# Reordering a fused attention and long-convolution kernel: the long kernel's transform ahead of the v projections, its spectra beside the logits

## The chip, the cores and the metric

The kernel runs on one core of one Trainium2 chip. The metric is the device time of one execution in microseconds (us). Times are medians over several executions of the same build, each beside executions of the kernel before on the same chip. Engine names in the profile: PE is TensorE (matmuls), PEld its weight loads, DVE is VectorE, ACT is ScalarE, POOL is GpSimd, SP is SyncE (here only a DMA queue). L582 means line 582 of the kernel source. In the traces here an engine's work stands in compiled order behind whatever waits ahead of it (DVE once for 8.84 us, below), and this matters for all that follows.

## The reference

Two unrelated computations share a launch, on sequences of 2048 rows with 576 columns:

```python
# A: dilated sliding-window attention, 32 heads of 18, window 8, dilation 2
q, k, v = split(x @ wqkv)
logits  = einsum("bhsd,bhswd->bhsw", q, k[idx]) * 18 ** -0.5   # idx = s - 2*w, masked below 0
o       = einsum("bhsw,bhswd->bhsd", softmax(logits), v[idx])
a       = o @ wo
# B: H3 long convolution
kv  = shift_conv4(k, shift_k) * v
y   = irfft(rfft(pad(kv)) * rfft(pad(ssm_k)))[:2048] + kv * ssm_D
b   = q * y
return concatenate([a, b], axis=-1)
```

`ssm_k` is called the long kernel below; it is as long as the sequence, so its transform costs as much as that of the data.

## The kernel before

The program is a string of 302 steps. Each step is `name.arguments:modifiers`; the modifiers choose which pair of PSUM buffers the step uses (`a` or `b`) and which engine copies the result out of PSUM (`s` ScalarE, `v` VectorE). A loop over the string emits instructions, and the framework's scheduler then fixes an order for each engine.

```python
for item in ORDER.split():
    item, _, mods = item.partition(":")
    name, *args = item.split(".")
    how["ps"] = next((m for m in mods if m in "ab"), None)   # PSUM pair
    how["ev"] = next((m for m in mods if m in "vs"), None)   # evacuating engine
    STEP[name](*map(int, args))
```

The steps that matter:

| step | what it does | lines |
|---|---|---|
| `v` | one of 16 v projections, ten matmuls | L380 |
| `lm`, `lb` | logit products on DVE; the sum of one of 8 groups on PE | L500, L516 |
| `kt`, `kp` | transpose of the long kernel and first transform stage, written to DRAM as `Dk` | L429 |
| `kl`, `xl` | load of a tile of `Dk` or `Dx` into a ring of slots | L568 |
| `ks`, `xs` | a spectrum: eight matmuls, four evacuations | L563 |
| `gp`, `gi` | spectral product on DVE; inverse stage on PE | L582, L596 |
| `pm`, `ps` | attention product on DVE; its sum on PE | L618, L632 |

A k spectrum has a tail that an x spectrum does not have. The product needs each half of it on the other half's partitions too, and two DMA copies on the POOL queue make that copy:

```python
def w_load(Dd, key, i):
    nc.sync.dma_start(Wr.get((key, i)), by_rt(Dd, i // 4, i % 4))

def k_spec(i):
    Kc = Kr.get(i)
    s2(Wr[("k", i)], i % 4, Kc[:, 0], 1.0 / 2048)      # matmuls and evacuations
    Wr.drop(("k", i))
    nc.gpsimd.dma_start(Kc[0:64, 1], Kc[64:128, 0])    # L574: the swap
    nc.gpsimd.dma_start(Kc[64:128, 1], Kc[0:64, 0])    # L575

def g_prod(i, hv):                                     # L582, needs Kc[:, 0] and Kc[:, 1]
    nc.vector.tensor_tensor(Pp.get((i, hv)), Kr[i][:, :, 4 * hv:4 * hv + 4, :],
                            Xr[i][:, 4 * hv:4 * hv + 4, :].unsqueeze(1).to_broadcast([128, 2, 4, HD]), ALU.mult)
```

In the string of before, all of `kl`, `ks`, `xl`, `xs` come behind the last group sum `lb.7`.

## Time and profile before

| | before |
|---|---|
| time, median of the first three executions | 253.45 us |
| span of the profiled execution | 251.1 us |
| PE busy | 222.8 us (89%) |
| DVE busy | 206.9 us (82%) |
| mean granted PE clock | 0.969 of full |

The prediction shows the page's busy shares and slices and the hole between 120 and 144 us. Two more views of the same run are needed. The first is the table of busy times over stages: window in us, its width, then busy time and instruction count of PE, PEld, DVE, ACT and POOL, the granted clock, the DMA share, and GB/s.

```profile
6.28:113.00 106.72, 104.11 (x799) 58.84 (x806) 100.26 (x118) 81.58 (x104) 5.49 (x18) 1.00 0.59 184
113.00:129.45 16.45, 14.53 (x132) 8.62 (x124) 12.42 (x16) 8.81 (x12) 1.49 (x2) 1.00 0.79 225
129.45:146.00 16.55, 8.21 (x44) 4.70 (x41) 11.80 (x13) 10.16 (x16) 1.08 (x2) 0.61 0.88 242
146.00:163.22 17.22, 15.42 (x180) 12.79 (x179) 13.26 (x13) 11.75 (x21) 2.05 (x4) 0.98 0.94 272
```

Subtract busy from width. PE has one bad row, the third: 8.3 us idle. DVE has three: 4.0, 4.8 and 4.0 us idle, 12.7 in all. The eye goes to PE's hole, since it is deep; DVE's is shallower and longer, and larger in sum.

The second is the list of waits: engine, line and what was waited for; then total us, how often, and the longest.

```profile
PE psB L563 <- DMA area<-Dx: 6.9, 2, 4.8
DVE area L582 <- DMA area<-area: 6.5, 4, 2.4
```

There are two candidates of the same size. PE waits for the load of `Dx`; DVE waits for the swap of a k spectrum. Nothing in these two lines says which of them sets the end. (Not all of DVE's idle time is the swap's: of the 4.8 us in the third row, 2.36 are put down to the swap and 2.03, ahead of the first attention product at 135.34 us, to another DMA between SBUF tiles, by its place a halo copy of v from the SP queue.)

### The profile page before, as it was taken

The page shows a single profiled execution, that of the slowest core. Times are in us where ns is not written, and L with a number is a line of the kernel's source. Part 1 is how long each engine was busy: PE and PEld are TensorE (multiplying, and loading weights), DVE is VectorE, ACT ScalarE, POOL GpSimd, SP SyncE. Part 2 cuts the span into 40 slices and gives each one's busy share as a digit, 9 for nine tenths or more (in the row PEclk, how much of TensorE's full clock was granted, in tenths as well). Part 3 has the DMA queues.
Part 4 walks back from the last instruction along what each step waited for, and adds up shares of the span by engine and source line. Part 5 has one row for each costly group of instructions (what it writes and reads, how often), then busy time and mean ns, then how long its engine had stood idle before and what let it go on. Part 6 is the DMA issues. An engine that isn't in the chain of part 4 may idle for free.

```text
span 251.1 us, 4991 instructions
## 1 busy us (share of the span) xinstructions
PE 222.8 (89%) x2007; PEld 150.5 (60%) x2013; DVE 206.9 (82%) x232; ACT 161.0 (64%) x231; POOL 25.4 (10%) x62
## 2 busy tenths in 40 slices
PE   1999899999999999999872599799999998999991
PEld 1346645445475549576531288667887786778881
DVE  2889999999997889998956679699889898966433
ACT  2878966765887756986645585688898653551120
POOL 8800000000000000002001011011120111111000
PEclk9999999999999999999996589999999999999998
DMA  6999994420336173918799779889978899968974
GB/s 206 328 337 373 357 310 125 162 87 28 94 97 188 27 210 94 273 33 241 210 223 318 226 196 283 276 244 271 287 234 228 291 247 255 322 212 263 276 228 141
DMA packets 44366, 55.24 MB, mean 220 GB/s; under 512 B 2316, under 2 KB 37468, under 8 KB 44344
## 3 DMA queue, kind: packets, MB, share of 16 engines
q1 hardware_dynamic: 42374, 47.71, 62.8%
q0 software_dynamic: 1968, 7.23, 10.7%
q8 instruction: 15, 0.25, 0.4%
q14 instruction: 7, 0.06, 0.1%
q10 hardware_dynamic: 2, 0.00, 0.0%
HBM read 29.27 MB, written 18.87 MB: 192 GB/s over the span
## 4 chain that ended last, share of the span: by engine, by line
PE 59%; DMA 10%; issue 10%; ACT 8%; DVE 7%; SPq 2%; POOL 1%; DVEq 0%; ACTq 0%; POOLq 0%
PE psA L393 10%; ACT area L96 8%; PE psA L380 7%; DMA area<-area 6%; PE psA L516 5%; PE psA L632 5%; PE psB L393 4%; PE psA L651 4%; PE psB L429 4%; PE psB L651 3%; DMA Dk<-area 2%; DVE area L618 2%; DMA area<-in_A_x_dram 2%; PE psB L596 2%; PE psB L632 1%
## 5 line engine op out<-in xcount | busy, mean ns | idle before, releaser
L96 ACT ACTIVATE area<-psB 128x576 bf16<-128x576 f32 (+6 forms) x124 | 84.6, 714 | 42.3 <-PE psB L563 13.4
L96 ACT ACTIVATE area<-psA 128x576 bf16<-128x576 f32 (+6 forms) x91 | 66.1, 753 | 38.7 <-PE psA L632 12.3
L618 DVE TENSOR_TENSOR area<-area,area 128x4096 bf16<-128x4096 bf16 x16 | 36.6, 2285 | 6.2 <-DMA area<-area 2.0
L500 DVE TENSOR_TENSOR area<-area 128x2048 bf16<-128x2048 bf16 x32 | 38.0, 1223 | 3.1 <-PE psA L516 3.1
L632 PEld LDWEIGHTS <-area 128*128 128x128 bf16 x512 | 32.6, 99 | 2.6 <-issue 0.5
L632 PE MATMUL psA<-ident,area 128*128 128x128 bf16 x448 | 32.0, 222 | 0.2 <-ACT area L96 0.2
L563 PE MATMUL psB<-area,W 128*128 128x288 bf16 x104 | 21.5, 306 | 9.4 <-DMA area<-Dx 6.9
L393 PEld LDWEIGHTS <-area 128*128 128x128 bf16 x160 | 15.8, 100 | 19.6 <-issue 3.2
L393 PE MATMUL psA<-area,area 128*128 128x512 bf16 x105 | 27.1, 401 | 0.2
L582 DVE TENSOR_TENSOR area<-area,area 128x2304 bf16<-128x2304 bf16 x16 | 21.2, 1350 | 6.5 <-DMA area<-area 6.5
L380 PEld LDWEIGHTS <-area 128*128 128x128 bf16 x160 | 19.7, 145 | 6.3 <-issue 5.7
L563 PEld LDWEIGHTS <-W 128*128 128x128 bf16 x128 | 12.6, 105 | 17.9 <-DMA area<-Dx 7.9
L380 PE MATMUL psA<-wv,area 128*128 128x288 bf16 x160 | 22.2, 288 | 0.9 <-ACT area L96 0.8
L460 DVE TENSOR_TENSOR area<-area,area 128x2304 bf16<-128x2304 bf16 x16 | 21.3, 1351 | 0.9 <-DMA area<-in_B_k_dram 0.8
L662 POOL DMA_DIRECT2D area<-in_B_q_dram x8 | 6.1, 765 | 133.9 <-DVE area L500 105.6
L651 PEld LDWEIGHTS <-area 128*128 128x128 bf16 x160 | 15.4, 97 | 5.8 <-issue 1.0
L429 PE MATMUL psB<-area,T 128*128 128x384 bf16 x74 | 17.2, 326 | 1.0 <-DVE area L290 0.4
L465 DVE TENSOR_TENSOR area<-area 128x2304 bf16<-128x2304 bf16 x12 | 16.2, 1352 | 0.2
L672 DVE TENSOR_TENSOR area<-psB,area 128x576 bf16<-128x576 f32 x13 | 9.6, 752 | 8.0 <-PE psB L671 5.7
L516 PE MATMUL psA<-area,Eh 128*32 128x512 bf16 x112 | 15.7, 632 | 0.0
L596 PEld LDWEIGHTS <-IAt 128*128 128x128 bf16 x128 | 12.2, 97 | 5.6 <-issue 2.5
L651 PE MATMUL psA<-wv,area 128*128 128x288 bf16 x90 | 13.3, 286 | 1.0 <-DVE area L98 0.7
(121 smaller groups left out, 274.2 us busy)
## 6 DMA issues: line engine op xcount, KB each, us to landing
Dx<-area SPq DMA_DIRECT2D x16, 288.0 KB, 3.0
Dk<-area SPq DMA_DIRECT2D x16, 288.0 KB, 4.4
area<-Dk SPq DMA_DIRECT2D x8, 576.0 KB, 4.9
area<-Dx SPq DMA_DIRECT2D x8, 576.0 KB, 5.6
area<-area POOLq DMA_DIRECT2D x16, 288.0 KB, 6.3
Dy<-area SPq DMA_DIRECT2D x8, 576.0 KB, 4.5
out_dram<-area SPq DMA_DIRECT2D x16, 288.0 KB, 4.6
area<-Dy SPq DMA_DIRECT2D x8, 576.0 KB, 6.6
```

The lines of the kernel that those rows point to most:

```text
L96: nc.scalar.activation(dst, src, ACT.Copy, **({} if scale is None else {"scale": scale}))
L380: nc.tensor.matmul(ps[:, di, 0:288], xTt[:, kb, t2, :], wv[:, kb, d0:d1], start=(kb == 0), stop=(kb == 4))
L393: nc.tensor.matmul(ps[:, u, :], wcols(kb, comp, 2 * cp + u), xT[:, kb, t], start=(kb == 0), stop=(kb == 4))
L429: nc.tensor.matmul(ps[:, ri, 0:384], T1[:, ri, :], sf[:, 384 * ch:384 * ch + 384], start=True, stop=not extra)
L460: nc.vector.tensor_tensor(dst, kfull[:, 4 * c + 3 - j:4 * c + 7 - j, :], skb[:, j, :].unsqueeze(1).to_broadcast([128, 4, D]), ALU.mult)
L500: nc.vector.tensor_tensor(dst[:, u], halves(q2[h], hf), halves(k2[h][:, :, shs[u]:shs[u] + S], hf), ALU.mult)
L516: nc.tensor.matmul(psw[32 * j:32 * j + 32, 0, :].rearrange("p (u a b) -> p u a b", u=2, b=2), Eh[:, 2 * h + c, :], prr[(n, h)][:, :, c, :, ...
L563: nc.tensor.matmul(ps[:, hp, 0:HD], W2[:, 8 * g + 2 * prl + hp].rearrange("p i l f -> p (i l f)"), Wt[:, 2 * prl + hp, :], start=True, sto ...
L582: nc.vector.tensor_tensor(Pp.get((i, hv)), Kr[i][:, :, 4 * hv:4 * hv + 4, :], Xr[i][:, 4 * hv:4 * hv + 4, :].unsqueeze(1).to_broadcast([12 ...
L618: nc.vector.tensor_tensor(P.rearrange("p w (d h) -> p w d h", h=H), vs[:, :, 0:16], at.to_broadcast([128, W, 16, H]), ALU.mult)
L632: nc.tensor.matmul(oaccs[tp][:, u, ct, :], P[:, wi, 128 * ct:128 * ct + 128], ident[:], start=(ct == 0 and wi == 0), stop=(wi == W - 1 and ...
L651: nc.tensor.matmul(ps[:, di, 0:288], lhs, wot[:, ct if ct < 4 else 4 + u, d0:d1], start=(ct == 0), stop=(ct == 4))
```

## The change

The intent is to end the transform of the long kernel early, beside the first logit groups, and to keep the v projections for later. Then loads and spectra (with their swaps) can be issued while logits are still summed, and PE has projections to fill the latency. The string is new throughout; its core is here, with cuts marked.

```diff
-lm.2.2 kp.1.2:s lb.2:s v.7:sa lm.3.1 lm.3.2 lm.4.0 kp.2.0:s kp.2.1:s lb.3:as kt.3:vb kp.2.2:a lm.4.1 v.6:a kt.4:bv
 [...]
-kp.6.1:sb kp.6.2:s v.14:s lm.6.1 kp.7.0:bs v.15:s kp.7.1:bs lm.6.2 lb.6:s lm.7.0 v.12:a lm.7.1 kp.7.2:b lwo ha.2 ha.3
-lm.7.2 lb.7:av kl.0 xl.0 ks.0:b kl.1 xl.1 xs.0 ks.1:a kl.2 pm.0.0 xs.1:b pm.0.1 xl.2 gp.0.0 gi.0.0 gp.0.1 ks.2:sb
+kp.7.1:s lm.3.2 lb.3:va sa.0 kp.7.2:b v.8:sb lm.4.0 v.4:as lm.4.1 lm.4.2 v.6:bs kl.0 v.5 kl.1 v.7 lm.5.0 lb.4:a lm.5.1
+lm.5.2 ks.0:bs lb.5:bs ha.1 v.11:a lm.6.0 sb.0 v.10:a ks.1:sa v.14:as xl.0 lm.6.1 v.12:bv v.13:va v.15:bs xl.1 v.9:sa
+lm.6.2 lb.6:av xs.1:b ha.2 lm.7.0 kl.2 ha.3 lm.7.1 at.0:s xs.0:sb lm.7.2 xl.2 lb.7 gp.0.0 gp.0.1 gi.0.0:b pm.0.0
 [... the rest of the string also changes in order, PSUM pair and evacuating engine]
-    Wr = Ring(mk.take(8, HD), mk.take(8, HD), wx)
+    Wr = Ring(mk.take(8, HD), mk.take(8, HD))
+    left = {f"v.{i}" for i in range(NT)} | {...all qk and qt steps...}
     for item in ORDER.split():
         [...]
+        left.discard(item)
+        if not left and len(Wr.slots) == 2:
+            Wr.slots.append(wx)
```

The last part is a matter of memory: the third load slot `wx` lies over the transposed x, which the projections read, so it joins the ring only when the last projection has been emitted.

More of the change, by code (lines that the diff above doesn't have):

```diff
@@ L18 @@
 ORDER = """
-lx.0 lwq.0 lx.2 xt.0.0:bs lx.1 sk:b lwq.1 xt.0.1:sa lkv.0 lkv.1 xt.0.2:v qk.0.1.0:bs cv.0 qk.0.0.0:sa lx.3 qk.1.0.0
-xt.1.0:bs xt.1.2:v lkv.2 xt.1.1:s qk.1.1.0:sa xt.2.0:a ia xt.2.2:s wt:s xt.3.2:va xt.3.0:b xt.3.1:sa sx.0.0:av cv.1
-sx.0.1:a sx.0.2:s qk.0.1.1 sx.1.0:b qk.0.0.1:a sx.1.1:sb sx.1.2:s lwv qk.1.0.1 cv.2 qk.1.0.3:sb xt.2.1:sa sx.2.0:sb
-lkv.3 sx.2.1:b qk.1.1.1:sa sx.2.2 sx.3.0:av qk.0.0.3:sb sx.3.1:v qt.0:bs qk.0.1.2:s sx.3.2:s qk.1.0.2:bs qk.1.1.2:av
-sx.4.0:s qk.0.0.2:sb cv.3 sx.4.1:b v.1:s qt.2:b sx.4.2:a qt.1:bs sx.5.0:b qk.0.1.3:s qk.1.1.3:sa sx.5.1 sx.5.2:v
@@ L24 @@
-qt.3:sa v.2:a v.0:a sx.6.0:a sx.6.1:sb sx.6.2:s lm.0.0 lm.0.1 sx.7.0:b lkn sx.7.1 kt.0:a lm.1.0 sx.7.2 lm.0.2 lb.0
-v.4:a lm.1.1 lm.2.0 kp.0.0:sb kp.0.1:a kt.1:s lm.1.2 lb.1:a lm.2.1 v.3:a kp.0.2:a kt.2:vb kp.1.0:as lm.3.0 kp.1.1:as
-lm.2.2 kp.1.2:s lb.2:s v.7:sa lm.3.1 lm.3.2 lm.4.0 kp.2.0:s kp.2.1:s lb.3:as kt.3:vb kp.2.2:a lm.4.1 v.6:a kt.4:bv
-kp.3.0:b v.5 ha.0 sa.0 kp.3.1:b kp.3.2:vb v.8:as kp.4.0:sb kp.4.1:s lm.4.2 kp.4.2:bs kt.5:v ha.1 sb.0 kt.6:a lb.4:as
-v.9:s v.10:s lm.5.0 v.11:a kp.5.0 kp.5.1:bs lm.5.1 lm.5.2 kp.5.2 kp.6.0:a at.0:s lb.5:bs kt.7:bv lm.6.0 v.13:va
@@ L29 @@
-kp.6.1:sb kp.6.2:s v.14:s lm.6.1 kp.7.0:bs v.15:s kp.7.1:bs lm.6.2 lb.6:s lm.7.0 v.12:a lm.7.1 kp.7.2:b lwo ha.2 ha.3
-lm.7.2 lb.7:av kl.0 xl.0 ks.0:b kl.1 xl.1 xs.0 ks.1:a kl.2 pm.0.0 xs.1:b pm.0.1 xl.2 gp.0.0 gi.0.0 gp.0.1 ks.2:sb
-xs.2:vb gp.1.0 xl.3 sa.1 xl.4 pm.1.0 gi.0.1:s gp.1.1 gp.2.0 ps.0.0:as ps.0.1:s ps.1.0:s xs.3 kl.3 ks.3:sb gi.1.0:bs
-kl.4 pm.1.1 gi.1.1:b ps.1.1:as gp.2.1 gp.3.0 pm.2.0 gi.2.0:av ks.4:s sb.1 xl.5 xs.4:s gi.2.1 po.0.0 kl.5 po.0.1:sb
-ps.2.0:v gp.3.1 gp.4.0 pm.2.1 ks.5:b ps.2.1:b po.1.0:bs pm.3.0 xs.5:a po.1.1:as gi.3.0:sb gi.3.1:bs kl.6 at.1 gp.4.1
@@ L34 @@
-pm.3.1 ps.3.0:a ps.3.1:a gi.4.0:sa pm.4.0 gi.4.1:sa gp.5.0 xl.6 ks.6:as xs.6:b yl.0 gp.5.1 pm.4.1 po.2.0:sb gp.6.0
-gi.5.0:v ys.0.0 pm.5.0 po.2.1:sa xl.7 kl.7 ks.7:v ps.4.0:as yl.1 pm.5.1 xs.7:sb po.3.0:v ps.4.1:sa ys.0.1:b po.3.1:sb
-yl.2 yl.3 gi.5.1:a ps.5.0:a pm.6.0 gp.6.1 gp.7.0 ys.1.0 ys.1.1 gi.6.0:bs gi.6.1:a ys.2.0:b ps.5.1:b gi.7.0:a ys.2.1
-gp.7.1 pm.6.1 po.4.0:sb gi.7.1:s yl.4 yl.5 ys.3.0:b po.4.1:v po.5.0:b ys.3.1:b ps.6.0:bv ps.6.1:av po.5.1:bs pm.7.0
-pm.7.1 po.6.0:s yl.6 ys.4.0:a ps.7.0:s ys.4.1 ys.5.0:a yl.7 po.6.1:av ys.5.1 ps.7.1:s ys.6.0:b po.7.0:a po.7.1:s
@@ L39 @@
-ys.6.1:b ys.7.0:b ys.7.1:a
+lx.0 xt.0.0:va xt.0.1:sa lx.1 lwq.0 sk:b lx.2 xt.0.2:a lwq.1 lkv.0 lkv.1 qk.0.0.0:sa qk.0.1.0:bs cv.0 lx.3 xt.1.2:sa
+xt.1.1:s lkv.2 xt.1.0:b qk.1.0.0:s ia:sb sx.0.0:b qk.1.1.0:sa xt.3.0 cv.1 sx.0.1:sa xt.2.0:a xt.3.2:v qk.0.0.1:av
+sx.0.2 xt.2.1:sb wt:s sx.1.0:bs sx.1.1:av qk.0.1.1:s xt.3.1:sb sx.1.2:as cv.2 qk.1.0.1:bs qt.0:bs sx.2.0:s xt.2.2:av
+sx.2.1:b lkv.3 qk.1.0.3 qk.0.0.3:sa sx.2.2:b sx.3.0:bs qk.1.1.1:as sx.3.1 lwv qk.0.1.2:a lkn qt.1:as sx.3.2:sb
+qk.1.0.2:s sx.4.0:bs qt.3 sx.4.1:av cv.3 sx.4.2:sb v.1:bs qt.2 v.2:sb sx.5.0:bv sx.5.1:as sx.5.2:as qk.0.0.2:b
@@ new lines @@
+qk.0.1.3:s sx.6.0:s sx.6.1 qk.1.1.3:a sx.6.2:b qk.1.1.2:b kt.0:a lm.0.0 sx.7.0:sa sx.7.1:v kp.0.0:sa sx.7.2:s kt.1:vb
+kp.0.1:sb kp.0.2:av v.0:sb kt.2:sa lm.0.1 lm.1.0 lm.0.2 kp.1.0:as kp.1.1:av kp.1.2:s lb.0:sb kp.2.0:a kp.2.1:s lm.1.1
+kt.3:v kp.2.2:as kp.3.0:s kt.4:va lm.1.2 kp.3.1:a lm.2.0 kp.3.2:sa lb.1:a kp.4.0:sb kp.4.1:s lm.2.1 kt.5:vb kp.4.2:a
+kp.5.0:bs kp.5.1:a kt.6:a kp.5.2 lm.2.2 lm.3.0 kt.7:s kp.6.0 kp.6.1:sb lb.2:s kp.6.2:s lm.3.1 kp.7.0:a v.3:b ha.0
+kp.7.1:s lm.3.2 lb.3:va sa.0 kp.7.2:b v.8:sb lm.4.0 v.4:as lm.4.1 lm.4.2 v.6:bs kl.0 v.5 kl.1 v.7 lm.5.0 lb.4:a lm.5.1
@@ new lines @@
+lm.5.2 ks.0:bs lb.5:bs ha.1 v.11:a lm.6.0 sb.0 v.10:a ks.1:sa v.14:as xl.0 lm.6.1 v.12:bv v.13:va v.15:bs xl.1 v.9:sa
+lm.6.2 lb.6:av xs.1:b ha.2 lm.7.0 kl.2 ha.3 lm.7.1 at.0:s xs.0:sb lm.7.2 xl.2 lb.7 gp.0.0 gp.0.1 gi.0.0:b pm.0.0
+gp.1.0 pm.0.1 ks.2:sa xs.2:vb ps.0.0:a gp.1.1 xl.3 gi.0.1:s pm.1.0 ps.0.1 gp.2.0 gi.1.0:sb kl.3 pm.1.1 kl.4 xs.3:b
+ps.1.0:as ks.3 xl.4 xl.5 lwo gp.2.1 pm.2.0 ps.1.1:b gi.1.1:a xs.4:s gi.2.0:vb kl.5 gi.2.1 gp.3.0 sa.1 sb.1 po.0.0:va
+po.0.1:sb pm.2.1 po.1.0:as gp.3.1 pm.3.0 ks.4:sb ps.2.0:a pm.3.1 kl.6 ks.5:sb gp.4.0 xs.5:a gi.3.0 po.1.1:b ps.2.1
@@ new lines @@
+gp.4.1 gi.3.1 at.1:bs yl.0 ps.3.0:av xl.6 ps.3.1:a gi.4.0:a gp.5.0 gi.4.1:sa pm.4.0 xs.6:bs po.2.0:bv ks.6:a gp.5.1
+gi.5.0:s pm.4.1 xl.7 ys.0.0:a gp.6.0 po.2.1:s ps.4.0:v kl.7 ks.7:b yl.1 po.3.0:sa po.3.1:a pm.5.0 xs.7 gp.6.1 ys.0.1:b
+ps.4.1:va ys.1.0:a gp.7.0 gi.5.1 yl.2 pm.5.1 ps.5.0:sa ys.1.1 ps.5.1 yl.3 pm.6.0 gi.6.0:sa ys.2.0 po.4.0:bs gi.6.1:s
+gi.7.0:as gp.7.1 gi.7.1:sa ys.2.1 pm.6.1 ys.3.0:a po.4.1:b yl.4 po.5.0:sb yl.5 ys.3.1:b ps.6.0:v pm.7.0 ps.6.1:bs
+po.5.1:sa ps.7.0:sa po.6.0:v ys.4.0:a pm.7.1 ys.4.1:a ps.7.1:av ys.5.0 ys.5.1:a po.6.1:sa po.7.0:s po.7.1:sb yl.6
@@ L40 @@
+ys.6.0:b yl.7 ys.6.1:a ys.7.0:a ys.7.1:b
 """
@@ L146, in __init__ @@
         def __init__(self, *slots):
-            self.slots, self.own, self.k = slots, {}, 0
+            self.slots, self.own, self.k = list(slots), {}, 0
         def get(self, key):
@@ L682 @@
                 ks=k_spec, xs=x_spec, gp=g_prod, gi=g_inv, pm=p_mul, ps=p_sum, po=p_out, yl=y_load, ys=y_step)
+    left = {f"v.{i}" for i in range(NT)} | {f"qk.{i}.{j}.{k}" for i in range(2) for j in range(2) for k in range(4)} \
+        | {f"qt.{i}" for i in range(4)}
     for item in ORDER.split():
```

## The prediction

> **What bounds the kernel now.** I read the page first: busy time by engine, then the slices.
>
> ```profile
> PE 222.8 (89%) x2007; PEld 150.5 (60%) x2013; DVE 206.9 (82%) x232; ACT 161.0 (64%) x231; POOL 25.4 (10%) x62
> ...
> PE   1999899999999999999872599799999998999991
> ...
> DVE  2889999999997889998956679699889898966433
> ...
> PEclk9999999999999999999996589999999999999998
> DMA  6999994420336173918799779889978899968974
> ```
>
> PE is busy 89% of 251.1 us and DVE 82%. Both run near full almost everywhere; the exception is a hole in slices 19 to 22 (120 to 144 us), where both sag together and the granted clock falls. The table of busy times over equal windows gives its size (columns: window, width, busy time of PE, PEld, DVE, ACT, POOL, clock, DMA share, GB/s):
>
> ```profile
> 119.27:125.55 6.28, 5.50 (x49) 3.48 (x48) 5.80 (x9) 3.90 (x6) 0.00 (x0) 1.00 0.72 209
> 125.55:131.83 6.28, 4.85 (x41) 2.06 (x38) 3.51 (x7) 2.82 (x6) 0.00 (x0) 1.00 0.91 224
> 131.83:138.10 6.27, 1.46 (x6) 0.82 (x7) 4.20 (x5) 3.35 (x4) 1.08 (x2) 0.60 1.03 318
> 138.10:144.38 6.28, 3.64 (x16) 1.84 (x15) 3.92 (x4) 3.27 (x7) 0.00 (x0) 0.50 0.79 225
> 144.38:150.66 6.28, 6.17 (x58) 5.06 (x57) 4.67 (x5) 5.50 (x10) 1.02 (x2) 0.81 0.75 196
> ```
>
> The timeline says what is waited for (start, duration, engine, line, then in brackets the idle time before and what ended it):
>
> ```profile
> 131.41 0.58 SPq L568 DMA_DIRECT2D area<-Dx  x1
> ...
> 132.54 0.55 POOL L574 DMA_DIRECT2D area<-area  x1 [13.30 <-ACT area L96]
> ...
> 136.38 1.14 PE L563 MATMUL psB<-area,W 128*128 128x288 bf16 x4 [4.82 <-DMA area<-Dx]
> ...
> 142.86 2.62 DVE L582 TENSOR_TENSOR area<-area,area 128x2304 bf16<-128x2304 bf16 x2 [2.36 <-DMA area<-area]
> ```
>
> Logits end (the last group sum on PE) at 129.45 us. Only then do the spectra (L563) start. The long kernel's transform wrote Dk until 122 us, its first tile is loaded from 124.86, and the first Dx load stands behind a halo copy in the SP queue until 131.41; PE waits for it until 136.38. The first k spectrum must also have its halves swapped by DMA (issued 132.54) before the first product at 142.86: over 10 us from issue to use. Nothing else was left for PE, since all v projections had been spent. The chain of waits agrees: it passes through the Dk write, the loads and "issue" between 112 and 147 us.
>
> **What the Trainium skill says.** "TensorE: Matmul & The Clock Gate", section "What's actually happening": the array runs at half rate by default and after an idle window of about 3.4 us, and at full rate after sustained work. The trace agrees: clock 0.60 and 0.50 around a 4.82 us wait, and four L563 matmuls take 1.14 us there, 0.65 us at 157.11. "DMA: Bandwidth & Descriptors", section "Issuing engines are not separate DMA queues": transfers from all issuers share the same 16 DMA engines and interleave. The trace agrees: the POOL-issued swaps, median 6.3 us to landing, take longest while SP's loads fill the DMA (share 1.03 in the window from 131.83). "Perfetto Trace Analysis", section "Optimization Strategy": regimes with different bounds gain from interleaving. Here the DMA share is 0.59 from 6.28 to 113 us and 0.87 to 0.88 after, so issuing loads earlier moves them to where there is room; whether it gains is what the change tests.
>
> **The change part by part.** No arithmetic is added or removed: the same 302 steps, 2013 matmuls and 4028 PE instructions in the compiled program of both. What differs is order, PSUM side and evacuation engine, and that the third load slot (it overlies x transposed) joins only when all q, k and v matmuls have been emitted, so that early loads take the two other slots.
>
> (1) Kernel transform earlier, v projections later. The eight transposes and 24 parts of the long kernel now end beside logits group 3, not group 7. When they end, 12 of the 16 v projections and four group sums are still to come. By 1.39 us for a v projection on the timeline (ten L380 matmuls; 1.3 where they run back to back) and 2.6 for a group sum (0.63 of L510 plus 2.0 of L516), PE has some 12 x 1.3 + 4 x 2.6 = 26 us of other work, against some 10 us of loading and swapping. Two Dk and two Dx loads and the spectra k0, k1, x1 and all but the last part of x0 come before group 7 is summed. In the compiled PE order the matmuls of k0 and k1 stand in pairs between pieces of v, so that ACT can evacuate one while PE works on the other. I expect this latency to vanish from PE's waits.
>
> (2) Idle PE before, from the windows: 5.2 us in the first 6.28; 2.6 up to 113; 1.9 from 113 to 129.45; 8.3 from 129.45 to 146; 1.8 to 163.2; 3.3 to 244.8; 5.1 at the end. Sum 28.2; with 222.8 busy it is the span.
>
> (3) Cold clock. From 129.45 to 146 PE was busy 8.2 us for 44 matmuls. Warm: 32 of L563 at 0.16 (four in 0.65 us) are 5.2 us, 12 of L632 at 0.056 (in 0.39 us groups of four they mostly overlap) 0.7; 5.9. Saved 2.3 us, if no gap as long remains. Busy becomes 220.5.
>
> (4) What remains at the turn. The compiled DVE order after the last logit product is four spectral products (4 x 1.35 = 5.4 us), a mask add (0.17), then the first attention product (2.29 + 0.42). So the first attention sum on PE can't start before 8.3 us after it. PE has for that time: last group sum 2.6, rest of x0 0.65, first inverse 1.33, k2 1.3, half of x2 0.65: 6.5 us, 1.8 idle. Then 1.9 us of sums, then a wait for the second attention product and for x2's evacuation, which is put on DVE behind it: 1.5 idle. I add 1.7, estimated, for the second product waiting on x0's evacuations (two of 0.65 on ACT). 5.0 in place of 8.3 + 1.8.
>
> (5) Run-up to the turn: the v projections and spectra are filler for PE while it waits for logit products, so I halve the 1.9 to 1.0.
>
> (6) Start: the second x block is now loaded ahead of wq. 576 KB at some 330 GB/s is 1.75 us; transposes fill a part. I charge 1.0.
>
> (7) More evacuation on DVE: counting copies in the compiled order up to the last logit product, x transposes +1.4 us, the copies of Dx, Dk, qk, v and logits +1.9, kernel transposes -0.8 (0.42 to 1.22 us each by the groups of before): +2.5 us. In this stretch DVE was busy 114.5 of 127 us, so it has 12.5 us of slack, 4.5 of it at the start. Charged 0, but it is why I don't go lower.
>
> Sum: 220.5 + 6.2 + 2.6 + 1.0 + 5.0 + 3.3 + 5.1 = 243.7 us span. Runs exceed the span by 253.45 - 251.1 = 2.35. Predicted 246.0 us, 2.9% faster.
>
> **The rivals.**
> (a) DVE takes over. Logits end 2.5 us later if DVE sets the pace from 18 to 75 us, where its windows are about 99% busy; PE too has four spectra more (about 5 us) before that point. And the first attention product comes about as late after the last logit product as before (8.3 us in both: 127.0 to 135.34). Then only the work moved ahead counts: some 2 to 4 us are gained, 249 to 251. For: both engines are nearly saturated in that stretch. Against: after the turn PE, not DVE, is 96% busy (78.26 of 81.60), and PE work there shrinks by the four spectra.
> (b) The hole vanishes wholly and DVE keeps up: turn 1.5 instead of 5, start 0, giving 241. For: the order looks searched, not hand-made. Against: the DVE order in (4).
> (c) DMA bound: share 0.88 after the turn. Two k and two x loads and the swaps move to before it, about 3.5 MB of some 30 MB (252 GB/s over 121.65 us), so a 6 us shorter stretch needs no higher rate. Worth 0 to 2 us against me; I give it little.
> (d) A wait of in-order queues: the x2 matmuls hold both psB buffers until DVE copies them, and wo is loaded later, in pieces between spectral loads in the SP queue, so the first output projection could wait. Each would cost 1 to 3 us: 247 to 249.
>
> **Range and chances.** (b) sets the low end, 240; (a) with (d) sets the high end, 251. The 2% line lies at 248.4, 2.4 us above my value, and (a) or (d) cross it alone: faster 0.66, same 0.31. Slower would need over 5 us lost in a schedule that only fills gaps: 0.03.
>
> **What would show it.** Right: in the windows from 120 to 150 us PE busy above 5.3 of 6.28 with clock 1.00; no L563 wait on Dx near 5 us; the swap's landing off the first spectral product; PE busy near 220.5; the last group sum ending later than 129.45, at 132 to 135. The remaining gap should be at the first attention sums, ended by DVE L618. Wrong: a second hole of over 4 us with the clock at 0.5 at the turn; first qk matmul over 2 us later than 9.23; or, after the turn, PE waiting repeatedly for DVE (a), or for DMA of Dk, Dx or wo (c, d).

## The result, and the profile after

Ratios here and below are the mean time of one kernel's fast runs over the mean of the other's fast runs of the same rounds, so they are not quite the ratio of the quoted medians.

| | before | after |
|---|---|---|
| time, median of 4 | 254.16 us (252.57 to 255.07) | 244.88 us (243.32 to 247.54) |
| span of the profiled execution | 251.1 us | 241.2 us |
| PE busy | 222.8 us | 219.0 us |
| DVE busy | 206.9 us | 205.9 us |
| mean granted clock | 0.969 | 0.996 |

The ratio is 0.9621 (95% interval 0.9539 to 0.9703): faster. One of after's four runs, 247.54 us, is marked slow (1.7% above the fastest) and is left out of the ratio. The profiled execution of after was the fastest of the four, so its span flatters it by some 1.5 us against the median; that of before (253.14 us) flatters it by 1.0. First the page of after, busy shares and slices:

```profile
PE 219.0 (91%) x2013; PEld 148.7 (62%) x2013; DVE 205.9 (85%) x232; ACT 159.4 (66%) x231; POOL 25.6 (11%) x62
...
PE   1998999999996998999999779999899999999991
...
DVE  1989999999988798998997999999999579974443
...
PEclk9999999999999999999999999999999999999999
DMA  6999994533435665557689887978879989879984
```

The 2-5-9 dip of PE is gone, the clock stays at 9, and DVE's fives and sixes in the middle have become nines. DMA, which swung between 0 and 9 tenths ahead of the hole, is loaded more evenly. The stages, in the same columns as before (the turn from logits to attention is the third and fourth row):

```profile
6.28:113.00 106.72, 101.98 (x787) 57.18 (x785) 99.59 (x121) 80.65 (x102) 5.51 (x18) 1.00 0.66 209
113.00:129.97 16.97, 16.43 (x147) 11.73 (x146) 16.76 (x23) 10.50 (x20) 2.30 (x5) 1.00 0.73 212
129.97:133.53 3.56, 3.56 (x32) 1.14 (x30) 2.53 (x2) 3.53 (x6) 1.35 (x2) 1.00 0.96 285
133.53:144.72 11.19, 7.86 (x84) 6.01 (x85) 11.03 (x13) 5.50 (x10) 1.08 (x2) 1.00 0.87 252
144.72:188.00 43.28, 41.19 (x442) 32.56 (x440) 42.22 (x40) 37.25 (x62) 4.64 (x8) 1.00 0.84 256
```

The third number of each row's busy times is DVE. From 113 to 144.72 us it is idle 0.21 + 1.03 + 0.16 = 1.4 us, where before it was idle for 12.7 us from 113 to 163. It then stays 98% busy to 188 us. PE keeps idle time at the turn, 3.3 us in the fourth row. The timeline of after (start, duration, engine, line, in brackets the wait before and what ended it) shows what happens there:

```profile
116.76 0.54 POOL L574 DMA_DIRECT2D area<-area  x1 [104.54 <-DVE area L539]
...
129.88 1.35 DVE L582 TENSOR_TENSOR area<-area,area 128x2304 bf16<-128x2304 bf16 x1
...
135.04 1.15 PE L596 MATMUL psB<-area,IAt 128*128 128x288 bf16 x8 [0.65 <-DVE area L582]
...
136.49 2.29 DVE L618 TENSOR_TENSOR area<-area,area 128x4096 bf16<-128x4096 bf16 x1
...
138.83 1.96 PE L632 MATMUL psA<-ident,area 128*128 128x128 bf16 x32
...
142.37 0.41 PE L563 MATMUL psB<-area,W 128*128 128x288 bf16 x2 [1.57 <-DVE area L98]
```

The swap of the first k spectrum is issued at 116.76 us, 13 us before its use. The first spectral product follows the last logit product without a wait, at 129.88 us instead of 142.86. Two of PE's three waits here end with DVE (L582, L98); the third, 0.96 us at 137.53, ends with copies by ACT. The list of waits of after says the same:

```profile
PE psB L563 <- DVE area L98: 1.6, 1, 1.6
...
DVE area L582 <- DMA area<-area: 1.1, 1, 1.1
```

Where did 9.9 us of span go? For any engine, busy plus idle is the span, so each engine has an account: PE lost 3.8 us busy and 6.1 idle; DVE lost 1.0 busy and 8.9 idle (44.2 to 35.3; 11.3 less in the middle, of which 1.7 are given back before 113 us and 0.8 later). Both accounts close, and so neither proves which engine mattered. That takes experiments.

### The profile page after: what moved, and what is told of

Its sections match the earlier page's. It is cut to its first block, busy times and chain, and to the rows that moved or that the text cites. A ratio compares the mean times of both kernels' runs of the same rounds, so it can differ in the third digit from the quotient of the medians.

```text
span 241.2 us, 4997 instructions
## 1 busy us (share of the span) xinstructions
PE 219.0 (91%) x2013; PEld 148.7 (62%) x2013; DVE 205.9 (85%) x232; ACT 159.4 (66%) x231; POOL 25.6 (11%) x62
## 4 chain that ended last, share of the span: by engine, by line
PE 65%; DVE 12%; ACT 12%; DMA 6%; issue 4%; DVEq 0%; SPq 0%; ACTq 0%
PE psA L393 11%; ACT area L96 8%; PE psA L632 7%; PE psA L651 4%; PE psB L380 4%; DVE area L618 4%; PE psB L429 3%; PE psA L516 3%; PE psB L563 3%; PE psB L651 3%; PE psA L380 3%; PE psB L596 3%; PE psB L393 3%; ACT IAt L96 3%; DVE area L500 2%
## 5 line engine op out<-in xcount | busy, mean ns | idle before, releaser
L96 ACT ACTIVATE area<-psB 128x576 bf16<-128x576 f32 (+6 forms) x121 | 82.3, 714 | 33.6 <-PE psB L596 10.3
L96 ACT ACTIVATE area<-psA 128x576 bf16<-128x576 f32 (+7 forms) x94 | 66.9, 739 | 38.4 <-PE psA L651 11.6
L618 DVE TENSOR_TENSOR area<-area,area 128x4096 bf16<-128x4096 bf16 x16 | 36.6, 2286 | 3.9 <-PE psA L632 3.3
L393 PE MATMUL psA<-area,area 128*128 128x512 bf16 x120 | 31.3, 399 | 0.3 <-ACT area L96 0.3
L582 DVE TENSOR_TENSOR area<-area,area 128x2304 bf16<-128x2304 bf16 x16 | 21.5, 1355 | 2.6 <-DMA area<-area 1.1
L574 POOL DMA_DIRECT2D area<-area x8 | 4.2, 527 | 159.0 <-DVE area L539 104.5
L563 PE MATMUL psB<-area,W 128*128 128x288 bf16 x96 | 18.0, 285 | 2.6 <-DVE area L98 1.6
L563 PEld LDWEIGHTS <-W 128*128 128x128 bf16 x128 | 11.9, 97 | 12.9 <-issue 10.0
L98 DVE CAST area<-psA 128x768 bf16<-128x768 f32 (+4 forms) x14 | 11.5, 834 | 6.3 <-PE psA L651 4.2
L429 PEld LDWEIGHTS <-T 128*128 128x128 bf16 x96 | 8.5, 98 | 12.9 <-issue 5.2
L429 PE MATMUL psB<-area,T 128*128 128x384 bf16 x60 | 14.0, 327 | 1.5 <-DVE area L290 1.2
L596 PE MATMUL psB<-area,IAt 128*128 128x288 bf16 x80 | 12.5, 285 | 1.0 <-DVE area L582 0.7
L651 PE MATMUL psA<-wv,area 128*128 128x288 bf16 x90 | 13.1, 286 | 0.0
```

Of the source, the lines that this page charges most:

```text
L96: nc.scalar.activation(dst, src, ACT.Copy, **({} if scale is None else {"scale": scale}))
L393: nc.tensor.matmul(ps[:, u, :], wcols(kb, comp, 2 * cp + u), xT[:, kb, t], start=(kb == 0), stop=(kb == 4))
L429: nc.tensor.matmul(ps[:, ri, 0:384], T1[:, ri, :], sf[:, 384 * ch:384 * ch + 384], start=True, stop=not extra)
L563: nc.tensor.matmul(ps[:, hp, 0:HD], W2[:, 8 * g + 2 * prl + hp].rearrange("p i l f -> p (i l f)"), Wt[:, 2 * prl + hp, :], start=True, sto ...
L596: nc.tensor.matmul(ps[:, hp, 0:HD], IAt[:, zi, 8 * g + hl, :], Pp[(i, hv)][:, zi, hl % 4, :], start=(zi == 0), stop=(zi == 1))
L618: nc.vector.tensor_tensor(P.rearrange("p w (d h) -> p w d h", h=H), vs[:, :, 0:16], at.to_broadcast([128, W, 16, H]), ALU.mult)
```

## The experiments

Theory T is the prediction's: at the turn PE waited for the `Dx` load and then ran on a cold clock; the change removes both. Rival R: what counted was DVE, standing in order before L582 until the swap had landed; PE's wait and its clock were beside the path. Rival F: the gain is not of this place at all but of the new string as a whole, of its fit of order, PSUM pairs and evacuating engines. Except where said, outputs were right.

**gate_loads: undo the early loads alone.** After, but the first loads and spectra stand behind `lb.7` in the string, and a tiny DVE copy from a logit of group 6 into each slot holds the loads back.

```diff
-[...] v.6:bs kl.0 v.5 kl.1 v.7 [...] ks.0:bs [...] ks.1:sa v.14:as xl.0 [...] xl.1 [...] xs.1:b [...] xs.0:sb
+[...] lm.7.2 lb.7 gl.0 gl.1 kl.0 xl.0 ks.0:bs kl.1 xl.1 xs.0:sb ks.1:sa kl.2 xs.1:b xl.2 gp.0.0 gp.0.1 [...]
+    def gate(i):   # step gl
+        nc.vector.tensor_copy(Wr.slots[i][0:1, 0, 0:1], Lh[1][0:1, 4, 0:1])
```

> The changed kernel with its first Dk and Dx loads held back until logits group 6 is evacuated, so that the spectra again follow group 7 on PE. Theory (the gain is the load-and-swap latency taken off PE's path): the hole comes back, PE waits several us for Dx or Dk with the clock near 0.5, 250 to 255 us. Rival (the gain comes from the rest of the new order, its PSUM sides and evacuation engines): at most 247 us.

Measured 257.28 us, ratio to before 1.0122 (1.0056 to 1.0188). The gain is gone and more. The stage table shows the hole back:

```profile
129.45:146.00 16.55, 9.50 (x57) 4.49 (x58) 11.30 (x14) 11.09 (x19) 2.94 (x6) 0.74 0.92 297
```

PE is idle 7.0 us at a clock of 0.74, and DVE's product waits 7.3 us for the swap, in five waits. It came out above the expected range, and the trace shows two likely reasons: the gate's copy stood on DVE behind the last logit product, so the loads were issued at 131.31 us, later than before's first one (124.86), and the first attention product was ready at 136.9 us, but PE's compiled order had spectra first, and its first attention sum came at 150.65. So in this string the gain goes when loads and spectra come late. Which of loads and swaps, this run can't tell.

**gate_spectra: early loads, late spectra.** The two Dk loads stay early; the spectra (and so the swaps, and the Dx loads that need their slots) are held back in the same way.

```diff
-lm.5.2 ks.0:bs lb.5:bs [...] ks.1:sa v.14:as xl.0 [...] xl.1 [...] xs.1:b [...] xs.0:sb lm.7.2 xl.2 lb.7 gp.0.0 [...]
+lm.5.2 lb.5:bs [...] lm.7.2 lb.7 gk.0 gk.1 ks.0:bs ks.1:sa xl.0 xl.1 kl.2 xs.1:b xs.0:sb xl.2 gp.0.0 [...]
+    def gate_w(key, i):   # step gk: adds 0 * logit to the loaded tile
+        [...]
+        nc.vector.tensor_tensor(w, w, t, ALU.add)
```

> The changed kernel with the two k loads early as they are, but the first spectra held back until logits group 6 is evacuated. Theory: the load of k is hidden, the swap and the x loads aren't, so part of the hole returns: 247 to 251 us, less than with the loads held back too. Rival (only the loads count): within 1 us of the changed kernel, 244 to 246. Rival (the rest of the order): the same 244 to 246 and no new wait at the first spectral product.

Measured 259.42 us, ratio 1.0229 (1.0182 to 1.0277): a miss, slower than gate_loads, although two loads were early. The list of waits:

```profile
DVE area L583 <- DMA area<-area: 11.3, 5, 6.6
```

DVE stands 11.3 us for swaps (its line 583 is L582 of the others). Early loads without early swaps are worth nothing here, though the gate itself is part of the loss: it let the first spectrum start at 134.46 us, 5 us later than in before. This was the first mark against T.

**b_by_hand: the named idea alone, put into before.** Before's string with the transform of the long kernel moved up, v moved back, two loads and two spectra early; all steps keep their own PSUM pair and engine.

```diff
-[...] lm.2.0 kp.0.0:sb kp.0.1:a kt.1:s [...] v.7:sa [...] kp.7.2:b lwo ha.2 ha.3 lm.7.2 lb.7:av kl.0 xl.0 ks.0:b kl.1 [...]
+[...] kp.7.0:bs lm.5.0 kp.7.1:bs kp.7.2:b v.4:a lm.5.1 lm.5.2 v.3:a kl.0 kl.1 ha.0 v.7:sa at.0:s lb.5:bs v.6:a ks.0:b
+lm.6.0 v.5 ha.1 v.8:as ks.1:a xl.0 xl.1 v.9:s [...] kl.2 xs.0 xs.1:b ha.3 lwo lm.7.2 xl.2 lb.7:av gp.0.0 [...]
```

> The kernel before with only the move made by hand: kernel transform ahead of the v projections, two loads and spectra k0, k1 early, its own PSUM sides and evacuation engines kept. Theory: at least half of the 9 us gain, 245 to 249 us. Rival (the gain needs the whole new order): 251 us or more.

Measured 260.71 us, ratio 1.0279 (1.022 to 1.0339): a clear miss in the other direction. The stage table and the list of waits:

```profile
129.45:146.00 16.55, 15.49 (x125) 9.53 (x124) 5.28 (x6) 9.19 (x15) 0.49 (x1) 1.00 0.97 239
```

```profile
DVE area L98 <- PE psA L380: 8.8, 1, 8.8
```

PE's hole is filled and its clock is full, just what T asks for, and the kernel is slower. DVE is busy only 5.28 us of that window: one v evacuation (L98) had been placed on it early in its order and stood 8.84 us for its projection, to 132.98 us, with all later DVE work behind it; another L98 then stood 5.78 us for a group sum, to 143.85. Filling PE's hole is not enough; this is a reason to look at DVE, and it shows that the idea does not work without a fitting choice of engines (F).

**a_order_b_sides: the new order with the old sides.** After's order, but each step with the modifiers that it had in before.

```diff
-lx.0 xt.0.0:va xt.0.1:sa lx.1 lwq.0 sk:b lx.2 xt.0.2:a lwq.1 [...]
+lx.0 xt.0.0:bs xt.0.1:sa lx.1 lwq.0 sk:b lx.2 xt.0.2:v lwq.1 [...]
```

> The changed order with each step's PSUM side and evacuation engine as in the kernel before. Theory (placement is what counts): 244 to 248 us. Rival (the new sides and engines carry the gain): 251 us or more.

Measured 259.8 us, ratio 1.0229 (1.0175 to 1.0282). Again the turn is good (PE 15.74 of 16.55 us from 129.45 at clock 1.00), but the stage ahead lost it: from 6.28 to 113 us PE was busy 95.05 us, against 101.98 in after. Of these 6.9 us, 3.2 are spectral parts that waited for ACT to free their PSUM pair:

```profile
PE psB L429 <- ACT area L96: 3.2, 7, 1.0
```

So F holds as a condition: order and sides must be found together. It does not say what the gain consists of.

**b_no_load, b_no_swap, b_no_both: take the latencies out of before.** Before's string, with the first two k and x loads, or the first two swaps, or both, not issued. The first spectra are then wrong on purpose; the comparison over the whole output did not notice, but these are no candidates. The edits:

```diff
 # b_no_load
-        nc.sync.dma_start(Wr.get((key, i)), by_rt(Dd, i // 4, i % 4))
+        w = Wr.get((key, i)); i > 1 and nc.sync.dma_start(w, by_rt(Dd, i // 4, i % 4))
 # b_no_swap
-        nc.gpsimd.dma_start(Kc[0:64, 1], Kc[64:128, 0])
-        nc.gpsimd.dma_start(Kc[64:128, 1], Kc[0:64, 0])
+        i > 1 and nc.gpsimd.dma_start(Kc[0:64, 1], Kc[64:128, 0])
+        i > 1 and nc.gpsimd.dma_start(Kc[64:128, 1], Kc[0:64, 0])
```

> The kernel before without the loads of k0, x0, k1 and x1 (the spectra read what lies in the slots; a wrong result on purpose). Theory (the turn's hole is load plus swap latency): the 4.82 us wait on Dx goes, the swap's wait stays, 249 to 252 us. Rival (a hole at the turn comes from DVE being late with attention products): 253 us, PE idle there unchanged but put down to DVE.

> The kernel before without the swaps of k0 and k1 (a wrong result on purpose), loads kept. Theory: the first spectral product no longer waits for DMA, but PE's wait on Dx stays, 250 to 252.5 us. Rival (only the swap counts): 248 us or less.

> The kernel before without both (a wrong result on purpose). Everything ahead of the turn stays in the same compiled order. Theory: it shows what the early issue can be worth by itself: idle PE from 129 to 146 us falls from 8.3 to 2 to 4 us, the clock stays at 1.00, 244 to 248 us. Rival (the gain comes from elsewhere in the new order): 251 us or more.

| kernel | median us | ratio to before, 95% |
|---|---|---|
| b_no_load | 255.20 | 1.0145 (1.0109 to 1.0181) |
| b_no_swap | 249.15 | 0.9838 (0.9785 to 0.9890) |
| b_no_both | 247.17 | 0.9741 (0.9695 to 0.9788) |

Before's median beside them was 253.29 us over 43 runs; 27 of these are marked slow because the fastest took 249.24, and the ratios use the others. With the means of all runs the three ratios are 1.007, 0.982 and 0.975, so their order does not hang on the marks. Without loads, the wait that the prediction put first, PE's for `Dx`, is gone, and the kernel is slower (249 to 252 us was expected: a miss). Its list of waits:

```profile
DVE area L582 <- DMA area<-area: 12.8, 5, 5.4
...
PE psA L632 <- DVE area L618: 8.1, 1, 8.1
```

One caution: with other load times the scheduler put four spectral products on DVE ahead of the first attention product, where before has two attention products first. So this run is not a clean removal of one wait; in it DVE meets the swap earlier in its order, and waits longer. Without swaps, the timeline shows:

```profile
135.30 1.14 PE L563 MATMUL psB<-area,W 128*128 128x288 bf16 x4 [4.07 <-DMA area<-Dx]
...
139.28 2.62 DVE L582 TENSOR_TENSOR area<-area,area 128x2304 bf16<-128x2304 bf16 x2
```

PE still waits 4.07 us for `Dx`, yet the kernel is 1.6% faster (249.15 us, between the ranges of both theories), and the first spectral product starts 3.6 us sooner than before's 142.86, without a wait. The run speaks for R, but alone it does not decide: with the swaps, PE's second wait for `Dx` (2.05 us at 142.65 in before) went too, the clock of the window from 129.45 us rose from 0.61 to 0.90, and from 144 us on the scheduler drew two spectral products forward on DVE. With both gone the time is another 2.0 us lower, although PE's clock in the window from 129.45 is only 0.79 there; DVE is busy 14.99 of the 16.55 us.

```profile
129.45:146.00 16.55, 12.95 (x87) 7.48 (x84) 14.99 (x15) 13.39 (x21) 1.08 (x2) 0.79 0.64 185
```

b_no_both has the compiled order of b_no_load, not that of before or of b_no_swap. That makes b_no_load and b_no_both the clean pair: in their traces PE, DVE and ACT run the same instructions in the same order, neither has the four loads, and only the two swaps differ. Without the swaps the time falls from 255.20 to 247.17 us, by 8.0 us, and DVE's waits for swaps from 12.8 to 4.1 us:

```profile
DVE area L582 <- DMA area<-area: 4.1, 2, 3.2
```

So in this order the swap, met on DVE, costs about what it is waited for, with no wait for these loads on PE in either run. That is R. What the pair can't separate is the traffic of the swaps, which goes with them (DMA share in the window from 129.45 us: 0.87 and 0.64).

**b_filler: keep PE warm, leave the waits.** Before, with 29 matmuls on constants placed in PE's hole. Nothing reads them.

```diff
-lm.7.2 lb.7:av kl.0 xl.0 ks.0:b kl.1 xl.1 xs.0 ks.1:a kl.2 [...]
+lm.7.2 lb.7:av kl.0 xl.0 ks.0:b fl.20 kl.1 xl.1 xs.0 ks.1:a fl.9 kl.2 [...]
+    def filler(n):
+        ps = psa()
+        for k in range(n):
+            nc.tensor.matmul(ps[:, k % 2, :], ident[:], W2[:, 0:4].rearrange("p h i l f -> p (h i l f)"), start=True, stop=True)
```

> The kernel before with 29 matmuls on constants put into the hole (20 after spectrum k0, 9 after k1), so that PE isn't idle there; the waits stay. It measures the cold clock. By step 3 of the prediction, 2.3 us: 250.5 to 252 us, clock above 0.95 from 132 to 146 us. Rival (the slow matmuls stand beside waits for DMA and cost nothing): 253 to 254.5 us.

Measured 253.76 us over 22 runs, ratio 1.0022 (0.9996 to 1.0048): no gain.

```profile
129.45:146.00 16.55, 11.83 (x61) 5.74 (x55) 12.20 (x13) 10.45 (x16) 1.47 (x3) 0.85 0.88 243
```

The window's clock rose from 0.61 to 0.85 and PE's busy time, fillers included, from 8.21 to 11.83 us; the time stayed. The array was not warm throughout (above 0.95 was expected), and from 151 us on DVE's order differs by one product, so the run bounds the clock's worth rather than measures it at zero; but of the 2.3 us that the prediction credited, nothing shows.

**b_loads_first: issue the first loads earlier, with right data.** Before, with the two first loads ahead of wo and the halo copies in the SP queue.

```diff
-[...] lm.7.1 kp.7.2:b lwo ha.2 ha.3 lm.7.2 lb.7:av kl.0 xl.0 ks.0:b [...]
+[...] lm.7.1 kp.7.2:b kl.0 xl.0 lwo ha.2 ha.3 lm.7.2 lb.7:av ks.0:b [...]
```

> The kernel before with the first Dx load issued ahead of wo and the halos in the SP queue. Theory as it now stands (DVE's wait for the swap sets the turn, not PE's wait on Dx): PE's 4.82 us wait on Dx shrinks below 2 us and the time stays within 1.5 us of before, 252 to 254.5 us. Rival (the prediction's reading, PE's wait on Dx is on the path): 249.5 us or less.

Measured 255.98 us, ratio 1.0115 (1.0046 to 1.0184), before's median beside it 253.26: above both ranges. The timeline, the stage table and the list of waits:

```profile
131.92 0.66 PE L563 MATMUL psB<-area,W 128*128 128x288 bf16 x4 [0.48 <-DMA area<-Dx]
...
143.46 2.63 DVE L582 TENSOR_TENSOR area<-area,area 128x2304 bf16<-128x2304 bf16 x2 [10.27 <-DMA area<-Dx]
```

```profile
129.45:146.00 16.55, 6.18 (x28) 2.88 (x26) 6.04 (x8) 9.90 (x15) 1.47 (x3) 0.70 0.87 216
```

```profile
PE psA L563 <- DMA area<-Dk: 5.6, 1, 5.6
```

PE's wait of 4.82 us has shrunk to 0.48, and the first product comes at 143.46 us, no earlier than before's. Here too the scheduler moved two spectral products ahead of the attention products, and DVE stood 10.27 us with them. (The bracket names the DMA that ended last by the profile.) PE's hole was not filled: a wait of 5.6 us for `Dk` took the place of the one that went, and PE was busy 6.18 us of the window, less than before's 8.21. So the move cost 1.1%, but what PE's wait for `Dx` is worth by itself this run does not show.

**a_no_both: take the same latencies out of after.** The edit of b_no_both, in after (wrong on purpose again). The compiled order of PE, DVE and ACT is the same as after's, so this one is clean.

> The changed kernel without the loads of k0, x0, k1, x1 and without the swaps of k0 and k1 (a wrong result on purpose; the compiled order of PE, DVE and ACT is the same to the instruction). The same edit took 2.6% off the kernel before. Theory (the change hides this latency): within 1 us of the changed kernel, 243.5 to 246 us. Rival (part of it still counts): 242.5 us or less.

Measured 243.80 us, ratio to before 0.9669 (0.9577 to 0.9761); after itself had 244.88 and 0.9621. The turn's row:

```profile
133.53:144.72 11.19, 7.97 (x87) 5.76 (x81) 11.03 (x13) 5.60 (x10) 1.08 (x2) 1.00 0.85 253
```

It answers to the row of after almost digit by digit. An edit worth 2.6% in before is worth nothing that the intervals can tell in after: the latency of these first loads and swaps is hidden there.

**a_x2_act: relieve the engine that is full.** After, with one x spectrum evacuated by ACT instead of DVE, since PE waits 1.57 us for that DVE copy.

```diff
-gp.1.0 pm.0.1 ks.2:sa xs.2:vb ps.0.0:a [...]
+gp.1.0 pm.0.1 ks.2:sa xs.2:sb ps.0.0:a [...]
```

> The changed kernel with spectrum x2 evacuated by ACT instead of DVE. Theory (after the turn DVE is the bound, busy without a break from 135 to 168 us): its four copies, 2.75 us, come off the path, the time falls by 1.5 to 3 us to 242 to 243.5. Rival (PE is the bound after the turn): within 0.8 us of the changed kernel, 244 to 245.7 us.

Measured 247.86 us, ratio to before 0.9801 (0.9737 to 0.9865): a miss, some 3 us slower than after. The timeline:

```profile
149.40 1.36 DVE L582 TENSOR_TENSOR area<-area,area 128x2304 bf16<-128x2304 bf16 x1 [5.12 <-ACT area L96]
```

Less work on DVE, but now in its order a product stands 5.12 us for a copy that ACT reaches late; from 144.72 to 188 us DVE is busy 36.12 us instead of 42.22. The experiment agrees with DVE's idle time being what counts at this place, and shows that moving work off a full engine can create such idle time.

## Why the prediction was right or wrong

The size was right: 246.0 us predicted with a range of 240 to 251, 244.88 measured; 2.9% predicted, 3.8% measured. The mechanism was right in half, and that the sum came so close is in part luck, as the table shows. The profile lets the sum be checked term by term (span of the profiled execution of after; idle terms are PE's):

| term | predicted | measured |
|---|---|---|
| PE busy | 220.5 | 219.05 |
| start, to 6.28 | 6.2 | 5.08 |
| 6.28 to 113 | 2.6 | 4.74 |
| run-up, 113 to last logit product | 1.0 | 0.54 |
| turn, to 150.75 | 5.0 | 3.5 |
| later, to 234.90 | 3.3 | 3.16 |
| end | 5.1 | 5.09 |
| sum | 243.7 | 241.2 |

(The prediction then added 2.35 us from span to time. The profiled execution of before took 253.14 us itself, so the right figure was 2.0; in after it is 2.1.)

- **Step (1), latency vanishes: right, and shown.** The swap is issued at 116.76 us, PE's waits for loads of `Dk` and `Dx` come to 0.2 us in all, and a_no_both gives the same time as after within the intervals.
- **What bounds the turn: the step that failed.** The prediction named PE's wait for `Dx` and "the swap's halves" in one breath, and charged the turn as PE's idle time plus a cold clock. What the runs show in its place is DVE, which stood in order for the swap: taking the swaps away is worth 8.0 us from b_no_load to b_no_both, and 1.6% in b_no_swap, which keeps before's order up to the first products, with a first `Dx` wait of 4.07 us still there; a warmer clock gained nothing (b_filler); and b_by_hand filled PE's hole and lost. PE's 4.82 us wait for `Dx` had time to spare at the first product. In before, ACT copied out the part of the x spectrum that the product reads with

```profile
137.08 1.19 ACT L96 ACTIVATE area<-psB 128x576 bf16<-128x576 f32 x2 [1.76 <-PE psB L563]
```

  that is by 138.27 us; DVE was free at 140.50, and the product started only at 142.86, when the swap had landed. The prediction also read the chain of waits as agreeing with its view. From 131 us on, that chain goes through the loads' issues and then the POOL queue's swaps into DVE's product, and no PE instruction is on it before 167 us ("issue" is time in which the profile shows no wait):

```profile
132.57 1.05 DMA area<-Dx
133.62 12.43 issue
146.04 0.47 POOL area L574
...
152.01 0.50 POOL area L574
152.52 7.12 DMA area<-area
159.92 1.19 issue
161.10 1.28 DVE area L582
```

  PE's waits are not proved worthless by this. In before the second half of spectrum k1 stood on PE behind x1, which waited 2.05 us for its `Dx` load, and k1's swap was issued only after it, at 146.04 us: a wait of PE can count by making a swap late. No run isolates that.
- **Step (3), cold clock 2.3 us: no gain shown.** PE's busy time did fall, by 3.8 us, more than the 2.3 credited; but b_filler, with the clock of the window at 0.85, was no faster. Where the other 1.5 us come from was not looked into.
- **Step (4), the turn: right in kind, too high by 1.5 us.** Two of the waits are the predicted ones: the first inverse waits 0.65 us for DVE's product, the x2 matmuls 1.57 us for their copy on DVE (1.5 predicted). A third, 0.96 us of k2's matmuls for ACT's copies, was not foreseen. The first attention sum starts 8.9 us after the last logit product (at least 8.3 predicted). Of the 1.7 us added for the second product waiting on evacuations, the trace shows 1.03 us ahead of it, which it puts down to issue, and 0.15 behind ACT's copies ahead of the fourth.
- **Step (5), run-up halved to 1.0:** 0.54 measured, 0.5 less than charged.
- **Step (6), start charged 1.0:** wrong. The first qk matmul starts at 9.23 us in both kernels, and the idle stretch ahead of it even shrank from 5.17 to 5.08.
- **Step (7), more evacuation charged 0:** wrong by some 2 us. In the stretch to 113 us PE is idle 4.74 us instead of 2.61. The timeline of after shows one of the new waits:

```profile
76.04 0.81 ACT L96 ACTIVATE area<-psA 128x768 bf16<-128x768 f32 x1 [2.01 <-DMA Dx<-area]
...
76.90 0.78 PE L479 MATMUL psA<-ident,area 128*128 128x128 bf16 x10 [1.85 <-ACT area L96]
```

  ACT waits for a staging buffer until its write to `Dx` is out, and PE waits for ACT: not DVE's slack, which the step had looked at, but a buffer. The 2.1 us too little here, 1.5 too much in (4) and 1.1 too much in (6) nearly cancel, which is luck.
- **The rivals.** (a) said that DVE takes over, and it does, in the turn and up to 188 us; but 9.3 us were gained and not 2 to 4. One of its readings was wrong: "8.3 us in both" sets the start of the first attention product in before against the earliest start of the first attention sum in after. On the traces the product starts 8.3 us after the last logit product in before and 6.5 in after, the sum 18.0 and 8.9. "PE, not DVE, is 96% busy after the turn" was read in before over a stretch of 82 us; in after, from 144.72 to 188, DVE is 98% busy and PE 95%. (c) and (d) left little: PE's waits for loads of Dk, Dx and wo are at most 0.5 us each in the list.
- **The signs.** Those for "right" came in part: PE busy 219.05 us, the last group sum's end at 133.53, the swap landed before its product, no long wait for `Dx`. But PE is busy only 4.28 and 4.46 of 6.03 us in the windows from 132.66 and 138.69 us, where over 5.3 of 6.28 was forecast, and the gaps there end with L582, L96 and L98, not with L618.

What stays open: b_no_both (247.17 us) and after (244.88) still differ by some 2.3 us. DVE's idle time in the run-up, 4.0 us in before and 0.2 in after, is a likely place, and so is its 2.03 us wait for a halo copy, which is gone in after; but no run isolates either; a_order_b_sides and b_by_hand show only that sides and order matter by more than that.

## What to carry to other kernels

When two engines have a hole at the same place, don't charge the deeper one: take away each wait by itself, and see which of them moves the end. Then compare only runs whose compiled order is the same: b_no_load, b_no_swap, b_no_both, b_filler and b_loads_first all changed more of the order than their edit says, and only b_no_load against b_no_both, and a_no_both against after, are free of it. A latency chain (load, matmul, evacuation, swap, product) should be planned back from its last link, so that its last DMA lands before the in-order engine that needs it gets there. And changing order without the engines and buffers that go with it, or the other way around, can lose more than the idea gains: here 2 to 3% lost against 3.8% won.

## What the Trainium skill lacked or had wrong

- "TensorE: Matmul & The Clock Gate", section "Terms", puts the penalty of a cold array at the throttled time times the missing share of the clock. By that rule before loses (1 - 0.969) x 251.1 = 7.8 us, an estimate. With the mean clock at 0.982 (b_filler) it would lose 4.5, but the ratio was 1.0022: the cold time that went was no lost time in this kernel. The page does not say that this can be; its half-rate itself agrees with the trace (four L563 matmuls in 1.14 us cold, 0.65 warm).
- "Perfetto Trace Analysis", section "Identifying the Most-Contended Engine", warns that matmul busy time is a poor measure of how near TensorE is to its limit, and names the share of peak arithmetic (MFU) and the busy share of weight loads instead. This case agrees: PE showed 89% and 91%, but weight loads only 60% and 62%, less than DVE's 82% and 85%. By weight loads (MFU was not worked out) DVE comes first, which the prediction, going by PE's 89%, passed over. What the page lacks is a test for gaps of two engines at one place: its search for gaps (section "Optimization Strategy") starts once the engine is known, and here runs were needed (b_no_load against b_no_both 8.0 us, b_filler 1.0022).
- No page that I consulted gives the latency of a swap of partition halves within SBUF beside other transfers: 288 KB per half took a median of 6.3 us from issue to landing in before and 5.3 in after, and the first swap of before some 10 us (issued at 132.54, used at 142.86) with a DMA share of 1.03 in the window from 131.83.
- No page that I consulted shows what one early-placed evacuation costs on an in-order engine: 8.8 us of DVE in b_by_hand, and 5.12 us in a_x2_act for a product placed ahead of its input.
